# A retention-and-Gelu kernel: the Gelu table loaded at launch, the copies of states spread over ScalarE, VectorE or both, and the casts reordered to match

## The chip, the cores and the metric

One core of a Trainium2 chip. The metric is the device time of one execution in microseconds (us); a kernel's time is the median of several executions. The *span* is what the profiler saw between the first and the last instruction; it is some 1.8 us shorter than the device time. Beside each execution stands the mean clock that was granted to TensorE, where 1.0 is full speed. Times are compared only between executions taken on the same chip. Profiles of several calls, from three chips or more, are set side by side in one table and in some means below; these are compared by stretches, and how far two executions of one kernel differ is shown beside them.

## The reference

```python
# B=8, H=8, S=576, D=64; x becomes 4608 x 512, w_in 512 x 2048, w_out 2048 x 512
def _attn_ref(q, k, v):
    scores = (1 / sqrt(D)) * q @ k.T
    gamma = 1.0 - 2.0 ** (-5.0 - arange(H))
    ret = scores * where(rel >= 0, gamma ** rel, 0.0)      # decay by distance, causal
    return ret @ v

def _moe_ref(x, w_in, w_out):
    h = x @ w_in
    g = 0.5 * h * (1 + tanh(sqrt(2 / pi) * (h + 0.044715 * h ** 3)))
    return g @ w_out

# reference: attention, heads side by side as x, then the two layers
# (the text is shortened: shapes as comments, no type conversions)
```

## The kernel before

The sequence of a batch entry is cut into chunks of 128 rows. What lies within a chunk is computed as scores, a mask and values (`score_mm`, `mask_sc`, `values`); what comes from earlier chunks goes through a state (`state_mm`, then `scan` on VectorE), which is copied by `put` into a block-diagonal float16 tile `tbd` and used by `inter_mm`. `evac` turns the result into `x`. `up` is the first layer with Gelu on ScalarE, `down` the second, as seven products instead of eight with sums and differences prepared by the `mix_` functions.

The program is a list of units of TensorE work; `plan` says after which unit each further step is issued. An instruction queue of an engine runs in the order of issue, so a plan entry decides the place in every queue at once. The letter at the end of an entry is the engine: A is ScalarE, V VectorE, G GpSimd, and S2 splits a copy between A and V.

```python
    def gelu_table():
        nc.scalar.activation(out=p2[:, 3:4], in_=p2[:, 2:3], func=AF.Gelu_apprx_tanh)
# ... cut ...
    def tr(b, s, hh, i, eng):                 # transpose k or q, evacuate to T
        a = att[b]
        t = bank("tr", F16)
        pad(("tr", b, s, hh, i), t)           # dummy matmuls that keep TensorE busy
        # ... cut: four transposes ...
        for e, gs in ((eng, slice(0, 4)),) if eng is not S2 else ((A, slice(0, 2)), (V, slice(2, 4))):
            copy(e, a["T"][:, s, hh, i, gs], src[:, gs])
# ... cut ...
    def put(b, n, eng=None):
        w = att[b]["w", n]
        for hl in range(2):
            copy(eng or nc.scalar, tbd[b % 2][half[hl], n, :, half[hl]], w[half[hl]])
# ... cut ...
    plan = add({},
        (0, L(mask)),
        (0, L(tbd_zero, 0, V)),
        (0, L(cast_qk, 0, 0, 0, "k", A)),
        (0, L(cast_qk, 0, 0, 0, "q", V)),
        (4, L(gelu_table)),
        (0, L(tr, 0, 0, 0, 1, S2)),
        (1, L(score_mm, 0, 0, 0)),
        # ... cut ...
        (8, L(scan, 0, 2)),
        (8, L(put, 0, 2)),
        (8, L(cast_w_in, 0, 1, G)),
        (8, L(cast_w_in, 0, 2, G)),
        (8, L(cast_w_in, 0, 3, G)),
        (8, L(values, 0, 1)),
        (8, L(F0.up_half, 0, 0)),
        (9, L(inter_mm, 0, 1, 1)),
        (10, L(F0.up_half, 1, 0)),
        # ... cut ...
        (78, L(put, 4, 3)),
    )
```

## Time and profile before

| | before |
|---|---|
| median of the first 3 executions | 302.81 us (302.34 to 303.06) |
| span of the profiled execution | 299.4 us |
| first score / last score of the first batch entry | 7.40 / 17.94 us |
| first long run of `up_half` matmuls | 23.43 us |
| first 512-column `up` matmul | 26.05 us |
| first product with w_out | 57.81 us |
| last matmul | 295.69 us |

The events are start times of matmuls, read from the trace. They cut the execution into stretches.

The view of TensorE's waits of the kernel before, from 26 to 128 us (columns: who waited, for whom, total us, how many times, the longest):

```profile
PE hp L555 <- ACT gT L559: 0.5, 1, 0.5
PE st L368 <- ACT T L233: 0.5, 1, 0.5
PE st L368 <- DVE T L233: 0.5, 1, 0.5
PE mu L625 <- DVE ret L381: 0.2, 1, 0.2
PE tr L325 <- DVE vs L446: 0.2, 1, 0.2
```

Only 1.9 us are listed in this long stretch. The first line is the wait at 126 us that the prediction's step (7) is about. Here is its cause, in order of time (columns: start, us, engine, line, operation, what from what; in brackets the idle time before and what ended it):

```profile
123.10 2.52 ACT L233 CAST tbd<-ws 64x256 f16<-64x256 f32 x6 [0.64 <-DVE ws L449]
...
125.64 0.60 ACT L559 ACTIVATE gT<-hp 128x512 f16<-128x512 f32 x1
126.29 3.89 PE L555 MATMUL hp<-x,w_in_sb 128*128 128x512 f16 x16 [0.51 <-ACT gT L559]
```

Six half copies of states stand in ScalarE's queue ahead of a Gelu, and the matmul at 126.29 waits for that Gelu.

### The profile page before, as it was taken

The numbers are of one execution on the slowest core, as the hardware profiler recorded it, in microseconds if no ns is written. First come the engines' busy times: TensorE is split into PE (matmuls) and PEld (weight loads), VectorE is DVE, ScalarE is ACT, GpSimd is POOL, SyncE is SP. The second block draws the span as 40 slices with busy tenths as digits, with TensorE's granted clock in tenths as the row PEclk, the third lists the DMA queues.
The fourth block names the chain that finished last, engine by engine and source line by source line (L and its number), as shares of the span: only waits on it lengthen the run. The fifth ranks groups of instructions, "written<-read, shape, count | busy, mean of one in ns | idle before, by whom it ended". The sixth has DMA issues, their size and how long they took to land.

```text
span 299.4 us, 8730 instructions
## 1 busy us (share of the span) xinstructions
PE 289.7 (97%) x3700; PEld 205.0 (68%) x3700; DVE 218.2 (73%) x416; ACT 163.3 (55%) x318; POOL 79.7 (27%) x108
## 2 busy tenths in 40 slices
PE   8888999999999999999999999999999999999995
PEld 6775577888885568655875587558755874784484
DVE  4776899999998995899559755975598353543434
ACT  6556888875556782665445544554355226505620
POOL 2663564474240343094046006500000000000000
PEclk9999999999999999999999999999999999999999
DMA  7999999758979999985895999491110021003204
GB/s 207 305 337 330 321 387 317 195 131 209 220 235 217 310 237 220 254 276 108 220 308 152 134 258 267 118 137 25 77 66 2 2 83 59 2 1 76 67 0 142
DMA packets 94711, 52.48 MB, mean 175 GB/s; under 512 B 38352, under 2 KB 88528, under 8 KB 94672
## 3 DMA queue, kind: packets, MB, share of 16 engines
q1 hardware_dynamic: 94336, 51.26, 64.4%
q10 hardware_dynamic: 336, 0.66, 0.8%
q8 instruction: 29, 0.48, 0.6%
q14 instruction: 10, 0.08, 0.1%
HBM read 36.70 MB, written 9.44 MB: 154 GB/s over the span
## 4 chain that ended last, share of the span: by engine, by line
PE 76%; DVE 14%; ACT 6%; DMA 2%; issue 1%; DVEq 0%; ACTq 0%
PE hp L555 32%; PE mz L625 8%; PE my L625 8%; PE mu L625 5%; PE mv L625 5%; PE mw L625 4%; PE xs L467 2%; PE hp L568 2%; PE st L368 2%; DMA ld<-in_k_dram 2%; DVE ret L381 2%; DVE ost L652 2%; PE xs L494 2%; ACT tbd L233 2%; DVE w_out_sb L296 1%; ACT gT L559 1%
## 5 line engine op out<-in xcount | busy, mean ns | idle before, releaser
L559 ACT ACTIVATE gT<-hp 128x512 f16<-128x512 f32 x124 | 73.6, 597 | 63.7 <-PE hp L555 62.9
L555 PE MATMUL hp<-x,w_in_sb 128*128 128x512 f16 x432 | 98.7, 379 | 0.6 <-ACT gT L559 0.5
L555 PEld LDWEIGHTS <-w_in_sb 128*128 128x128 f16 x496 | 47.1, 98 | 52.1 <-issue 1.0
L625 PEld LDWEIGHTS <-gT 128*128 128x128 f16 x576 | 55.8, 98 | 8.0
L381 DVE TENSOR_TENSOR ret<-st,cm 128x512 f16<-128x512 f32 x64 | 40.8, 693 | 2.2 <-PE st L368 2.2
L242 POOL TENSOR_TENSOR cv<-ld,sc 128x512 f16<-128x512 f32 x27 | 30.3, 1133 | 28.6 <-DMA ld<-in_v_dram 16.8
L233 ACT CAST tbd<-ws 64x256 f16<-64x256 f32 x64 | 25.8, 403 | 22.2 <-DVE ws L449 19.4
L233 POOL CAST kq<-ld 128x512 f16<-128x512 f32 x24 | 19.4, 810 | 62.0 <-DMA ld<-in_k_dram 46.0
L593 DVE TENSOR_TENSOR gsum<-gT 128x1024 f16<-128x1024 f16 x36 | 26.7, 740 | 12.3 <-ACT gT L559 12.3
L625 PE MATMUL mz<-w_out_sb,gT 128*128 128x256 f16 x288 | 34.4, 273 | 0.0
L625 PE MATMUL my<-w_out_sb,gT 128*128 128x256 f16 x288 | 34.4, 273 | 0.0
L625 PEld LDWEIGHTS <-gsum 128*128 128x128 f16 x288 | 28.0, 98 | 3.5
L652 DVE TENSOR_TENSOR ost<-ost,mv 128x512 f32<-128x512 f32 x18 | 11.5, 682 | 22.3 <-PE mv L625 19.6
L597 DVE TENSOR_TENSOR gT<-gT 128x1024 f16<-128x1024 f16 x36 | 26.9, 751 | 0.5
L507 DVE TENSOR_TENSOR x<-xs,gx 128x512 f16<-128x512 f32 x32 | 21.8, 685 | 6.5 <-PE xs L494 6.4
L585 DVE TENSOR_TENSOR gdia<-gT 128x512 f16<-128x512 f16 (+1 forms) x34 | 17.9, 527 | 10.1 <-ACT gT L559 7.5
L568 PE MATMUL hp<-x,w_in_sb 128*128 128x256 f16 x160 | 18.9, 273 | 0.8 <-DVE x L507 0.8
L233 ACT CAST kq<-ld 128x512 f16<-128x512 f32 x30 | 18.1, 616 | 1.0 <-DMA ld<-in_q_dram 0.7
L625 PE MATMUL mu<-w_out_sb,gsum 128*128 128x256 f16 x144 | 17.2, 273 | 0.2 <-DVE ret L381 0.2
L625 PE MATMUL mv<-w_out_sb,gsum 128*128 128x256 f16 x144 | 17.2, 273 | 0.0
L625 PE MATMUL mw<-w_out_sb,gdia 128*128 128x256 f16 x144 | 17.2, 273 | 0.0
L568 PEld LDWEIGHTS <-w_in_sb 128*128 128x128 f16 x160 | 15.2, 98 | 2.8 <-issue 0.9
(95 smaller groups left out, 319.8 us busy)
## 6 DMA issues: line engine op xcount, KB each, us to landing
ld<-in_k_dram SPq DMA_DIRECT2D x30, 256.0 KB, 5.3
ld<-in_q_dram SPq DMA_DIRECT2D x30, 256.0 KB, 5.3
ld<-in_v_dram SPq DMA_DIRECT2D x30, 256.0 KB, 5.5
out_dram<-ost SPq DMA_DIRECT2D x14, 512.0 KB, 4.6
loan<-in_moe_w_out_dram SPq DMA_DIRECT2D x12, 256.0 KB, 5.4
loan<-in_moe_w_in_dram SPq DMA_DIRECT2D x8, 256.0 KB, 6.1
ld<-in_moe_w_in_dram SPq DMA_DIRECT2D x8, 256.0 KB, 6.0
ld<-in_moe_w_out_dram SPq DMA_DIRECT2D x4, 256.0 KB, 5.6
```

The lines of the kernel that those rows point to most:

```text
L233: (eng.copy if eng is nc.scalar else eng.tensor_copy)(out=out, in_=in_)
L242: eng.tensor_tensor(out=unperm(att[b]["v"][:, s, hh, :]), in0=perm(t), in1=sc[:, 8 * hh : 8 * hh + 8] .rearrange("p (r h) -> p r h", r=2) ...
L381: nc.vector.tensor_tensor(out=x.rearrange("p (a m) -> p a m", a=2), in0=st[hl].rearrange("p (a m) -> p a m", a=2), in1=cm.rearrange("p r s ...
L507: nc.vector.tensor_tensor(out=xb[b][:, :, 2 * s + c].rearrange("p s q i -> p q s i"), in0=att[b]["x", s][c].rearrange("p (q s i) -> p q s ...
L555: nc.tensor.matmul(hp, w_in_sb[:, ct, 128 * f : 128 * f + 128], x[:, :, ct, :], start=(ct == 0), stop=(ct == 3),)
L559: nc.scalar.activation(out=self.g(f // 2)[:, f % 2], in_=hp, func=AF.Gelu_apprx_tanh)
L568: nc.tensor.matmul(hp[:, 256 * h : 256 * h + 256], w_in_sb[:, ct, 256 * j + 128 * h : 256 * j + 128 * h + 128], xb[self.b][:, :, 2 * u : 2 ...
L585: nc.vector.tensor_tensor(out=self.sa[:, j : j + n], in0=g[:, :, 0, 0:256], in1=g[:, :, 1, 256:512], op=ALU.add)
L593: nc.vector.tensor_tensor(out=self.sc[:, j : j + n], in0=g[:, :, 0], in1=g[:, :, 1], op=ALU.add)
L597: nc.vector.tensor_tensor(out=g.rearrange("p j h c -> p j (h c)")[:, :, 256:768].rearrange("p j (h c) -> p j h c", h=2), in0=g[:, :, :, 0: ...
L625: nc.tensor.matmul(o, lhs(j, slice(128 * u, 128 * u + 128)), w_out_sb[:, j, w], start=((u == 0 or isinstance(t, list)) and j == 0 and not ...
L652: nc.vector.tensor_tensor(out=out, in0=in0, in1=t, op=op)
```

## The change

Its intent is to clear ScalarE's queue in the first 27 us, where copies, casts and the table load stood in one row, to give VectorE and GpSimd a share of it, and to do the same for a few places later. It has five parts:

```diff
# 1. the Gelu table at launch; an early dummy Exp starts the Exp table load sooner
     nc.vector.memset(wz, 0.0)
+    nc.scalar.activation(out=p2[:, 3:4], in_=wz[:, 0:1], func=AF.Exp)
...
+    nc.scalar.activation(out=p2[:, 3:4], in_=wz[:, 0:1], func=AF.Gelu_apprx_tanh)
...
-    def gelu_table():
-        nc.scalar.activation(out=p2[:, 3:4], in_=p2[:, 2:3], func=AF.Gelu_apprx_tanh)

# 2. the copy of states names its engine and can be split
-    def put(b, n, eng=None):
+    def put(b, n, eng):
         w = att[b]["w", n]
         for hl in range(2):
-            copy(eng or nc.scalar, tbd[b % 2][half[hl], n, :, half[hl]], w[half[hl]])
+            e = (A, V)[hl] if eng is S2 else eng
+            copy(e, tbd[b % 2][half[hl], n, :, half[hl]], w[half[hl]])

# 3. the start (most entries cut)
+        (0, L(tbd_zero, 0, G)),
+        (0, L(cast_qk, 0, 0, 0, "q", G)),
...
-        (8, L(put, 0, 2)),
+        (8, L(put, 0, 2, V)),
+        (3, L(cast_w_in, 0, 3, A)),
-        (8, L(cast_w_in, 0, 3, G)),
+        (9, L(F0.up_half, 0, 0)),
-        (8, L(F0.up_half, 0, 0)),
...
# 4. casts and sums between 26 and 94 us (cut to three entries), and the last state copy
+        (10, L(cast_w_in, 1, 1, V)),
+        (18, L(cast_w_in, 3, 3, G)),
+        (16, L(cast_v, 1, 0, 0, G)),
...
-        (78, L(put, 4, 3)),
+        (78, L(put, 4, 3, S2)),

# 5. the loop over the later blocks: sums and differences
-            (12, L(F.mix_d, 2, 2)),
+            (13, L(F.mix_d, 2, 2, V)),
-            (11, L(F.mix_sa, 4, 2)),
+            (11, L(F.mix_sa, 4, 2, G)),
...
# and in the last two blocks, five of twelve on GpSimd
+                (4, L(F.mix_sc, 0, 2, G)),
+                (7, L(F.mix_d, 0, 2, G)),
+                (9, L(F.mix_d, 2, 2, G)),
+                (15, L(F.mix_sc, 6, 2, G)),
+                (15, L(F.mix_d, 6, 2, G)),
```

Cut: the order of the first loads, the numbers of dummy matmuls (116 become 128), many moves by one or two units, and a set of new functions (`forms_w`, `pair_a` and so on) that nothing calls, since the list of pairs to use them for is empty.

## The prediction

> **What bounds the kernel now.** I read the page first, then a table of windows by stage, then the chain of waits of the first 27 us, then who waited on TensorE, and last the order of time around each wait. The page's busy shares, with PE at the top:
>
> ```profile
> PE 289.7 (97%) x3700; PEld 205.0 (68%) x3700; DVE 218.2 (73%) x416; ACT 163.3 (55%) x318; POOL 79.7 (27%) x108
> ```
>
> 97% alone doesn't say that TensorE works usefully, so here are stages (columns: window, its length, then busy us and instruction count of PE, PEld, DVE, ACT, POOL, then clock, DMA share, GB/s):
>
> ```profile
> 7.40:15.00 7.60, 6.41 (x169) 5.52 (x170) 5.97 (x12) 4.07 (x8) 4.55 (x7) 1.00 1.10 306
> 15.00:22.00 7.00, 6.29 (x160) 5.11 (x157) 5.48 (x9) 3.46 (x8) 5.08 (x7) 1.00 1.05 334
> 54.00:64.00 10.00, 10.00 (x101) 8.94 (x98) 9.90 (x21) 8.91 (x20) 6.84 (x5) 1.00 0.60 162
> 64.00:78.00 14.00, 13.54 (x233) 11.82 (x232) 13.97 (x28) 6.60 (x15) 6.72 (x8) 1.00 0.80 202
> 154.00:184.00 30.00, 30.00 (x403) 20.40 (x401) 22.03 (x41) 15.78 (x30) 10.04 (x15) 1.00 0.90 213
> 244.00:270.00 26.00, 26.00 (x178) 17.19 (x177) 10.60 (x19) 11.32 (x19) 0.00 (x0) 1.00 0.11 42
> ```
>
> The reader should see three regimes. From 127 us to the last matmul TensorE is full. A block without attention takes 26.03 us, 64 matmuls of 512 columns (13.81 us in the chain of waits) and seven products (1.75 us each, 12.2 us); one with attention 29.9 us. No rearrangement of other engines shortens these 169 us. From 26 to 127 us TensorE has small holes and VectorE is close to full (9.90 of 10 us, 13.97 of 14). Before 26 us TensorE looks busy but does mostly padding: 16 warm-up matmuls (3.59 us) and 116 dummy matmuls of 128 columns, against real work that I estimate at 7.9 us from the counts and shapes. The DMA share there is above 1, at 306 to 334 GB/s. The start is a race between loads and a chain over ACT, DVE and PE:
>
> ```profile
> 11.38 1.28 DVE ret L381 x2
> 12.66 0.34 DVE ws L449
> 13.00 0.02 issue
> 13.02 0.40 ACT tbd L233
> 13.43 0.01 issue
> 13.44 0.40 ACT tbd L233
> 13.84 0.02 issue
> 13.87 0.63 ACT kq L233
> ...
> 14.97 0.59 ACT T L233
> 15.56 0.52 ACT kq L233
> 16.07 0.30 ACT tbd L233
> ...
> 22.08 1.31 DVE x L507 x2
> 23.39 0.04 issue
> 23.43 2.79 PE hp L568 x24
> ```
>
> From 13 to 18 us the chain lies on ScalarE: state copies (tbd), casts of k and q, evacuations of transposes. At 22 to 23.4 us it is two output evacuations on VectorE, behind a late state copy.
>
> **What the Trainium skill says.** "ScalarE: Activation LUTs", section "What ACT_TABLE_LOAD costs", gives about 1283 ns for the load, plus a drain. The trace agrees on the load and shows no separate drain:
>
> ```profile
> 10.76 1.28 ACT L134 ACT_TABLE_LOAD   x1
> 12.05 0.20 ACT L134 ACTIVATE p<-p 128x1 f32<-128x1 f32 x1
> 13.02 0.82 ACT L233 CAST tbd<-ws 64x256 f16<-64x256 f32 x2 [0.77 <-DVE ws L449]
> ```
>
> "TensorE: Matmul & The Clock Gate", section "Back-to-back issue gap", gives N/2.4 + 2.5 ns warm: 216 ns for 512 columns, 109 for 256. The blocks above give 13.81 us / 64 = 216 and 1.75 us / 16 = 109. So the late stages have no TensorE slack. "SBUF — State Buffer", section "Terms", says that VectorE and GpSimd share a port pair under an exclusive lock. The trace agrees as far as casts on GpSimd go: 614 ns undisturbed, but 810 on average over the 24 of the k/q group. "GPSIMD Engine Reference", section "4.1 Engine selection", puts two-input elementwise work at about twice VectorE's time; here the v cast is 1043 ns on GpSimd and 680 on VectorE, a factor of 1.5.
>
> **The change part by part.**
>
> (1) The Gelu table. It removes 1.28 + 0.20 = 1.48 us from ScalarE at 10.76 to 12.25. But the third line above says that ScalarE then idled 0.77 us for VectorE's state (ws), which waited for the mask (ret). The load was hidden: its own worth is 0. At launch, a dummy Exp lets the Exp table load at about 1.05 instead of 1.60, since it waits only for the zero tile. The four gx, sc and gt then end near 4.4 rather than 4.75, and the Gelu load and dummy occupy ScalarE until 5.9. That displaces the first k cast (4.65 on ScalarE).
>
> (2) First casts on GpSimd. After the cm iota (2.53) come four memsets (525 ns each, overlapping, 1.92 us on the trace), to about 4.5. The q cast runs when its load is there (4.80) to 5.4, k to 6.0. Before, both ended near 5.25. The transposes themselves started at 5.72 and 6.33, and the first score at 7.40. With q evacuated by ScalarE (0.59) and k split over both (0.38 and 0.28), I get the score at 7.3: no gain, no loss.
>
> (3) Second heads. Before, the k cast stood behind the first mask on VectorE (mask to 9.15, cast to 9.68) and two transposes followed it. Now k is cast ahead of the mask; only q is behind it (0.43), with one transpose and one evacuation. Four transposes less in series at 56 ns, and a shorter cast: about -0.4 us on the second score, 10.91 to 10.5.
>
> (4) The q cast of the second half moves from ScalarE (0.63 on the chain at 13.87) to GpSimd and can run at its load's landing, about 12.5. Its evacuation is split (-0.2). In return ScalarE takes a weight cast (0.62) after the first state copy. That takes back nearly the cast's share. Together with (3), the last score, 17.94 before, comes near 17.5.
>
> (5) State copy 2 on VectorE. ScalarE did it at 21.38, 0.82 us for two halves, and will now be blocked until about 21.7 by a weight tile that loads late. On VectorE two 64x256 casts cost, from its 128x256 w_out_sb cast at 0.30 us, an estimated 0.6. It delays VectorE's own evacuations, but one of these is no longer behind it: the product with state 1 is issued before the first half product. I estimate VectorE's last evacuation 0.5 us sooner relative to the score. With (3) and (4), the big matmuls begin at 22.5 instead of 23.43: -0.9.
>
> (6) From 26 to 45 us VectorE loses a k cast, a w_in cast (0.42 each), a v cast (0.69) and a q cast (0.79 on the trace), 2.3 us, and gains two w_in casts in its idle time (2.64 us at 24.2) and 0.15 of split evacuations. TensorE's hole at 33.96 (0.46 us wait plus refill) should close: -0.5.
>
> (7) The last state copy before the third block is split. ScalarE had six half copies in a row, 2.52 us, ahead of the Gelu activation at 125.64, for which TensorE waited 0.51 us (126.29). One half less is 0.40: -0.4.
>
> (8) Later blocks: one mix goes to GpSimd, five in the last two, and some subtractions move later. A 1024-element mix there would be 2.1 us by the v cast's rate (an estimate); the last block's two finish near 288.6, and the product that reads the second starts at 292.3. Effect 0. The subtraction moved behind the fourth product ends near 180.9 in the fifth block, 0.2 us before its reader: close, perhaps +0.1 in all.
>
> (9) 128 dummy matmuls instead of 116: 12 x 56 ns = 0.7 us, but inside waits. 0.
>
> Sum: -0.9 - 0.5 - 0.4 + 0.1 = -1.7, and some of it will be lost in the full VectorE stage: -1.6.
>
> **The rivals.** (a) Loads bound. The start's gain is swallowed since the DMA queues are full to 54 us and weights arrive no sooner; the same with VectorE, full from 54 to 94 us. For it: the chain has a 5.74 us load at 44.92, then VectorE work almost without a break to 64.5. Against: (6) relieves VectorE just before. It would give 302.3. (b) Head-of-line blocking. ScalarE has two w_in casts, GpSimd more casts, in queues that run in order; a tile 1 us late stalls TensorE. For it: GpSimd had waits of 4.50 us for w_in and 16.8 in all for v. Against: the load order was moved along with them. It would give 303.5 to 304.5. (c) The whole of the holes goes: the PE waits after 26 us, 3.3 us by summing the start-to-start excess of the larger gaps, and 1.5 at the start. That gives 298.5. (d) Gelu load on the path: 1.48 us more, 299.7; the 0.77 us idle speaks against it.
>
> **Range and chances.** Central 302.8 - 1.6 = 301.2 us. The range runs from between (c) and the sum, 299.5, to just under the time before, 302.8, which includes (a). Two per cent is 6.06 us. Faster by that needs under 296.8, beyond even (c); the start would have to shrink by four microseconds against full DMA queues. Slower by that needs 308.9, several blockings of type (b). Chances: 0.03 faster, 0.96 same, 0.01 slower.
>
> **What would show it.** Right: the table load before 6 us and no gain in the step where it was; second score near 10.5, last near 17.5, first big run of matmuls near 22.5; no TensorE wait near 33 us; the wait at 126 us halved; blocks at 29.9 and 26.03 us as before. Wrong: a TensorE wait for a cast on ACT or POOL between 18 and 36 us (b); the start of the first w_out product unchanged though the start moved (a); a late block longer than 30.0 us, which would put the fault in (8).

## The result, and the profile after

| | before | after |
|---|---|---|
| median | 302.72 us (302.34 to 303.06, 4 executions) | 299.92 us (299.71 to 300.52, 4 executions) |
| ratio of fast executions | | 0.9911 [0.9892, 0.9930] |
| span of the profiled execution | 299.4 us | 298.1 us |
| last matmul | 295.69 us | 294.40 us |

A ratio is the mean time of one kernel's fast executions over that of the other's of the same rounds, so not quite the ratio of the medians; in brackets is its 95% interval. The kernel is faster by 0.9%, within the 2% that counts as the same. Note a trap at once: by the medians it gained 2.8 us, but the two profiles differ by 1.3 us. The profiled execution of the kernel before took 301.22 us, less than any of its four timed ones.

The page of the kernel after, busy us by engine:

```profile
PE 289.9 (97%) x3712; PEld 205.0 (69%) x3712; DVE 217.2 (73%) x400; ACT 160.7 (54%) x316; POOL 108.1 (36%) x130
```

GpSimd works 28 us more, yet VectorE is relieved of only 1.0 us and ScalarE of 2.6. In the last blocks, what moved onto GpSimd slowed VectorE down, as is shown further below. The windows of the kernel after (columns as in the prediction):

```profile
7.40:15.00 7.60, 6.96 (x178) 6.21 (x167) 5.19 (x13) 2.59 (x7) 5.30 (x9) 1.00 1.16 314
...
64.00:78.00 14.00, 13.90 (x242) 12.06 (x243) 13.96 (x27) 6.23 (x14) 9.21 (x12) 1.00 0.97 240
...
244.00:270.00 26.00, 26.00 (x178) 17.16 (x177) 12.42 (x13) 11.28 (x20) 11.36 (x5) 1.00 0.11 42
```

From 7.4 to 15 us ScalarE goes from 4.07 us to 2.59 us of work. From 64 to 78 us VectorE is as full as before, 13.96 of 14 us. In the last window TensorE has no gap, before and after. ScalarE's order of time at the start of the kernel after:

```profile
3.99 1.28 ACT L125 ACT_TABLE_LOAD   x1
5.28 0.20 ACT L125 ACTIVATE p<-wz 128x1 f32<-128x1 f16 x1
5.80 0.99 ACT L232 COPY T<-tr 128x512 f16<-128x512 f16 x2 [0.32 <-PE tr L342]
9.24 0.59 ACT L232 COPY T<-tr 128x512 f16<-128x512 f16 x1 [2.45 <-PE tr L342]
```

The table load and its dummy end at 5.48 us, before ScalarE starts its first evacuation of transposes at 5.80; before the next one it waits 2.45 us for TensorE. The chain of waits up to the first long run, of the kernel after:

```profile
18.73 0.68 DVE ret L408
19.41 0.54 DVE w_in_sb L232
...
20.85 0.28 DVE tbd L232
...
21.15 0.29 DVE tbd L232
...
21.47 1.30 DVE x L535 x2
...
22.81 2.78 PE hp L669 x24
```

The link that was ScalarE's is now two copies of 0.28 and 0.29 us on VectorE, and the evacuations follow with no gap. But VectorE has become the chain from 18.73 us on: even a weight cast (0.54) stands in it.

TensorE's waits in the kernel after, from 26 to 140 us:

```profile
PE hp L669 <- DVE x L535: 0.3, 1, 0.3
PE hp L583 <- DVE ret L408: 0.2, 1, 0.2
PE us L459 <- POOL cv L241: 0.2, 1, 0.2
PE mu L726 <- DVE ret L408: 0.2, 1, 0.2
PE tr L352 <- DVE vs L473: 0.2, 1, 0.2
```

The three waits of 0.5 us are gone; three new ones of 0.2 and 0.3 us have come, and the two behind VectorE's `ret` and `vs` have stayed. At 126 us, now:

```profile
122.15 2.09 ACT L232 CAST tbd<-ws 64x256 f16<-64x256 f32 x5 [0.64 <-DVE ws L476]
...
124.06 0.29 DVE L232 CAST tbd<-ws 64x256 f16<-64x256 f32 x1
124.15 0.59 ACT L587 ACTIVATE gT<-hp 128x512 f16<-128x512 f32 x1
...
124.78 3.97 PE L583 MATMUL hp<-x,w_in_sb 128*128 128x512 f16 x17
```

Five half copies instead of six, the sixth beside them on VectorE; TensorE does not wait at all. One half copy (0.4 us) less was enough to remove a wait of 0.51.

From the first 512-column matmul on, the kernel after stood ahead by 0.62 us (26 us), 0.65 (57 us), 0.95 (105 us), 1.64 (128 us) and 1.29 us from 138 us to the end.

### The profile page after: what moved, and what is told of

Its sections match the earlier page's. It is cut to its first block, busy times and chain, and to the rows that moved or that the text cites. A ratio compares the mean times of both kernels' runs of the same rounds, so it can differ in the third digit from the quotient of the medians.

```text
span 298.1 us, 8776 instructions
## 1 busy us (share of the span) xinstructions
PE 289.9 (97%) x3712; PEld 205.0 (69%) x3712; DVE 217.2 (73%) x400; ACT 160.7 (54%) x316; POOL 108.1 (36%) x130
## 4 chain that ended last, share of the span: by engine, by line
PE 76%; DVE 13%; DMA 5%; SPq 3%; issue 1%; ACT 1%; DVEq 0%
PE hp L583 32%; PE mz L726 9%; PE my L726 9%; PE mu L726 5%; PE mw L726 5%; PE mv L726 4%; PE hp L669 3%; DVE ret L408 3%; DMA loan<-in_moe_w_in_dram 2%; SPq L188 2%; DMA ld<-in_moe_w_out_dram 2%; PE xs L495 2%; PE xs L522 2%; PE st L395 1%; DMA loan<-in_moe_w_out_dram 1%; DVE gT L698 1%
## 5 line engine op out<-in xcount | busy, mean ns | idle before, releaser
L583 PEld LDWEIGHTS <-w_in_sb 128*128 128x128 f16 x496 | 47.1, 98 | 51.8 <-issue 0.7
L232 POOL CAST kq<-ld 128x512 f16<-128x512 f32 x31 | 20.3, 664 | 57.5 <-DMA ld<-in_k_dram 43.2
L241 POOL TENSOR_TENSOR cv<-ld,sc 128x512 f16<-128x512 f32 x28 | 30.9, 1115 | 27.5 <-DMA ld<-in_v_dram 13.2
L232 ACT CAST tbd<-ws 64x256 f16<-64x256 f32 x61 | 24.6, 403 | 23.8 <-DVE ws L476 23.2
L694 DVE TENSOR_TENSOR gsum<-gT 128x1024 f16<-128x1024 f16 x32 | 25.5, 798 | 7.7 <-ACT gT L587 7.7
L694 POOL TENSOR_TENSOR gsum<-gT 128x1024 f16<-128x1024 f16 x4 | 9.2, 2300 | 36.4 <-ACT gT L587 36.4
L686 POOL TENSOR_TENSOR gdia<-gT 128x512 f16<-128x512 f16 x4 | 4.9, 1220 | 37.2 <-ACT gT L587 29.6
L669 PEld LDWEIGHTS <-w_in_sb 128*128 128x128 f16 x160 | 15.3, 98 | 3.4 <-issue 1.5
```

Of the source, the lines that this page charges most:

```text
L232: (eng.copy if eng is nc.scalar else eng.tensor_copy)(out=out, in_=in_)
L241: eng.tensor_tensor(out=unperm(att[b]["v"][:, s, hh, :]), in0=perm(t), in1=sc[:, 8 * hh : 8 * hh + 8] .rearrange("p (r h) -> p r h", r=2) ...
L583: nc.tensor.matmul(hp, w_in_sb[:, ct, 128 * f : 128 * f + 128], x[:, :, ct, :], start=(ct == 0), stop=(ct == 3),)
L669: nc.tensor.matmul(hp[:, 256 * h : 256 * h + 256], w_in_sb[:, ct, 256 * j + 128 * h : 256 * j + 128 * h + 128], xb[self.b][:, :, 2 * u : 2 ...
L686: e.tensor_tensor(out=self.sa[:, j : j + n], in0=g[:, :, 0, 0:256], in1=g[:, :, 1, 256:512], op=ALU.add)
L694: e.tensor_tensor(out=self.sc[:, j : j + n], in0=g[:, :, 0], in1=g[:, :, 1], op=ALU.add)
```

## The experiments

The theories. **By parts:** the start gives about 0.6 us, the split copy at 126 us 0.7 us, the rest of the middle nothing, the later blocks nothing. **Rival 1:** the early Gelu load by itself makes the gain. **Rival 2:** the two executions profiled differ mainly by luck at the start, and much of the 1.3 us is not the kernel's. In this section "before" in a result means the 11 executions of the kernel before on the same chip.

### The kernel before again, unchanged

No edit.

> The kernel before, unchanged: a control. Two profiled runs differ by 1.29 us in span (299.4 and 298.1) but the timed medians by 2.8 us (302.72 and 299.92). Theory A (the profile of before is a lucky execution; its usual span is about 300.9): ratio 1.000, all times 302.3 to 303.1, and the span of this run's profile near 300.9, with the extra 1.5 us at one place. Theory B (the timing of before outside the profile is longer by something after or before the span): ratio 1.000 and span 299.4 again at a time of 302.7.

Measured: 302.66 us (300.95 to 304.12, 6 executions) against 301.97 (301.25 to 302.29), ratio 1.0024 [0.9997, 1.0051]. One and the same kernel spreads over 3.2 us, and even its two sets of executions differ by 0.7 us in the median. Part of the spread lies at one place. TensorE of this execution, in order of time:

```profile
19.26 0.82 PE L467 MATMUL xs<-ret,cv 64*64 64x128 f16 x28
20.82 0.25 PE L467 MATMUL xs<-ret,cv 64*64 64x128 f16 x4 [0.74 <-issue]
21.00 1.05 PE L568 MATMUL hp<-x,w_in_sb 128*128 128x256 f16 x8
```

TensorE stops for 0.74 us after 28 of 32 matmuls of one product. Nothing is waited for ("issue"): these matmuls have all their data. In the profile of the first page the same pause, at the same matmul, is 0.21 us. It is taken up below with the merged dummies.

### The start alone

The kernel before, with the launch, the order of the first loads, the numbers of dummies and all entries up to unit 10 taken from the kernel after.

```diff
+        (8, L(put, 0, 2, V)),
+        (3, L(cast_w_in, 0, 3, A)),
...
# entries from unit 11 on, and the loop: as before
```

> Only the first stage of the change (launch, table load, loads of the first head group and of w_in, dummy matmuls, all steps up to unit 10); everything later as before. Theory C (the gain adds up by stages as the two profiles show): first long run of matmuls at 22.8, 0.6 us sooner, and the time 0.6 us shorter than before, ratio 0.998. Theory D (the 1.5 us that the profiles do not show sit in the start): ratio 0.993, nearly all of the gain. Theory E (the middle stage is bound by VectorE and loads): the start's 0.6 us are lost by 60 us, ratio 1.000.

Measured: 300.39 us, ratio 0.9951 [0.9935, 0.9966]. Its interval excludes 1: the start alone is worth 0.5%. Its profile, span 298.8 us, is ahead of the first profile of the kernel before by only 0.24 us at 26 us and by 0.62 us from 95 us on. Ahead of the profile of the kernel before from the same call it is by 0.74 us at 26 us, by 1.17 at 57 and by 1.48 at the last matmul. The wait at 126 us for a Gelu is still there.

### The middle alone

The kernel before with the entries of units 11 to 78, and the order of the loads behind those of w_in, from the kernel after.

```diff
# units up to 10: as before
...
+        (78, L(put, 4, 3, S2)),
# the loop: as before
```

> Only the steps of units 11 to 78 of the change (with the loads behind w_in), start and late blocks as before. Theory C: the holes at 47.8, 63.9 and 125.6 us close and some new ones open: 0.3 to 1.0 us shorter, ratio 0.998. Theory D: under 0.4 us, ratio 0.999. Theory E: all of the gain, ratio 0.992.

Measured: 300.93 us, ratio 0.9971 [0.9934, 1.0008], unclear by the times. In its profile the stretch with the wait at 126 us is 0.70 us shorter than before. The 31.7 us stretch from 26 to 57 us is not shorter (32.10 us), though the hole at 33 us is closed.

### The loop over the later blocks alone

```diff
-            (11, L(F.mix_sa, 4, 2)),
+            (11, L(F.mix_sa, 4, 2, G)),
...
# everything ahead of the loop: as before
```

> Only the loop over the later blocks as after the change (mixes on GpSimd and later, store later). By both profiles every block past 135 us takes the same time in both kernels, so all theories: ratio 1.000. If not, the 1.5 us lie there. The new TensorE hole of 0.36 us at 132 us should be there if it comes from the mix on GpSimd in the third block, and then the time is 0.3 us longer.

Measured: 301.87 us, ratio 1.0017 [0.9982, 1.0052]. No gain. From 138 us to the last matmul it takes 157.41 us, as does every other kernel.

### The kernel after again, unchanged

> The changed kernel again, as a control beside the controls of before. Theory C (the stage gains of the two single-stage runs, 0.9951 and 0.9971, add up): ratio 0.992, span 297.5 to 299. If it is nearer 0.996, the stages share one gain; nearer 0.988, the chip of the first comparison understated it.

Measured: 300.73 us (299.82 to 301.06, 6 executions) against 302.60 (301.09 to 305.53), ratio 0.9933 [0.9894, 0.9973]. The gain holds, at 0.7%. The ratios of the start alone and the middle alone multiply to 0.992, which lies between the two of the whole change. Here is the most useful table: stretches between the same matmuls in 14 profiles, worked out from start times in the traces (us). "26" is the start of the first 512-column matmul; the next columns are durations from there to the first product with w_out, to the 17th `up` matmul of the block that begins at 91.5 us in the kernel before (at about 95 us), to the 17th of the block that begins there at 123 us (about 127 us), to the 49th of the same block (about 138 us), and to the last matmul.

| kernel, execution | "26" | to 57 | to 95 | to 127 | to 138 | to end |
|---|---|---|---|---|---|---|
| before | 26.05 | 31.76 | 38.08 | 32.40 | 9.99 | 157.42 |
| before again | 26.55 | 31.71 | 38.26 | 32.64 | 9.99 | 157.41 |
| before, dummies merged | 25.91 | 31.83 | 38.25 | 32.40 | 9.99 | 157.42 |
| before, only the Gelu load moved (slow) | 30.74 | 31.38 | 38.44 | 32.81 | 9.99 | 157.42 |
| late part alone | 25.85 | 31.64 | 38.74 | 32.40 | 9.99 | 157.41 |
| start alone | 25.81 | 31.27 | 38.19 | 32.40 | 9.99 | 157.42 |
| middle alone | 25.80 | 32.10 | 38.36 | 31.70 | 9.99 | 157.42 |
| after | 25.43 | 31.73 | 37.78 | 31.70 | 10.34 | 157.41 |
| after again | 26.21 | 32.05 | 37.83 | 31.70 | 9.99 | 157.41 |
| after, state copy 2 on ScalarE | 27.03 | 31.39 | 37.84 | 31.70 | 9.99 | 157.41 |
| after, Gelu load back in the stream | 28.84 | 32.42 | 38.16 | 31.70 | 10.25 | 157.42 |
| after, three edits | 25.42 | 31.80 | 38.50 | 31.71 | 9.99 | 157.42 |
| after, last state copy unsplit | 25.34 | 31.69 | 38.16 | 32.40 | 9.99 | 157.42 |
| after, one mix later | 25.60 | 31.90 | 38.41 | 31.70 | 9.99 | 157.42 |

Three things are to be seen. The last column never moves by more than 0.01 us: no kernel here gains or loses after 138 us. The column "to 127" has two values, 32.40 without and 31.70 with the split copy, with two exceptions, 0.24 and 0.41 us longer, among those without. And the columns "to 57" and "to 95" differ by up to 0.3 us between two executions of one kernel, and by 0.6 to 0.7 ("to 95") among kernels with the same order there, as much as the holes that were to be closed.

That corrects a reading of the first pair of profiles. The wait at 132 us that appeared after the change ("to 138", 10.34 us) is not there when the same kernel runs again. In the first execution, in order of time:

```profile
130.25 1.22 POOL L241 TENSOR_TENSOR cv<-ld,sc 128x512 f16<-128x512 f32 x1
130.49 1.53 DVE L698 TENSOR_TENSOR gT<-gT 128x1024 f16<-128x1024 f16 x1
...
131.94 1.87 DVE L408 TENSOR_TENSOR ret<-st,cm 128x512 f16<-128x512 f32 x3
...
132.67 1.02 PE L583 MATMUL hp<-x,w_in_sb 128*128 128x512 f16 x4 [0.20 <-DVE ret L408]
```

and in the second, which runs 1.14 us later at this point:

```profile
131.61 1.09 DVE L698 TENSOR_TENSOR gT<-gT 128x1024 f16<-128x1024 f16 x1
...
132.12 2.48 POOL L241 TENSOR_TENSOR cv<-ld,sc 128x512 f16<-128x512 f32 x2
132.62 1.87 DVE L408 TENSOR_TENSOR ret<-st,cm 128x512 f16<-128x512 f32 x3
```

The same subtraction on VectorE took 1.53 us where GpSimd began a cast just ahead of it, and 1.09 us where that cast came later. The mask behind it ended in time, and TensorE did not wait. GpSimd's row of casts started at 125.12 us in the first execution and at 127.78 in the second, each time on the landing of a k load.

### The Gelu load alone

The kernel before with parts 1 and 2 of the diff, every copy on ScalarE as before. Four weight casts also changed their places in the list, to other places with the same engine.

```diff
+    nc.scalar.activation(out=p2[:, 3:4], in_=wz[:, 0:1], func=AF.Exp)
...
+    nc.scalar.activation(out=p2[:, 3:4], in_=wz[:, 0:1], func=AF.Gelu_apprx_tanh)
...
-        (4, L(gelu_table)),
```

> Before, with only the two launch-time table loads (dummy Exp and dummy Gelu) and without the step that loaded the Gelu table at unit 4. Theory F (the load was hidden behind the mask and the state on VectorE; my prediction): the second score stays within 0.2 us of 10.9, ratio 1.000 within 0.002; the first k cast on ScalarE moves from 4.65 to about 5.3, so the first score comes 0 to 0.6 us later. Theory G (the table load was on the path): first long run of matmuls 1 us sooner, ratio 0.996.

Measured: 301.62 us, ratio 0.9960 [0.9913, 1.0007], which leaves anything from nothing to 0.9% open. The profiled execution was a slow one (306.21 us, mean clock 0.989), so nothing is read from it after 20 us as a difference between kernels. Up to there it is undisturbed: the second score comes at 10.98 and the last at 18.01 us, against 10.91 and 17.94 before. Taking the load out of the old order moves no event up to there. So this trace gives rival 1 nothing to stand on at the place where the load was. The times can't exclude it: the fast executions at a clock of 0.998 or more have a mean span of 299.62 us against 300.39 for the kernel before.

What this slow execution lost can be seen in it, and that is worth a look though it is no difference between kernels. Windows of this execution (columns as before; the clock is the third number from the right):

```profile
20.00:25.00 5.00, 2.73 (x33) 2.16 (x24) 0.97 (x3) 1.40 (x3) 2.12 (x4) 0.80 1.07 334
25.00:30.00 5.00, 4.05 (x24) 2.91 (x22) 2.50 (x4) 0.60 (x1) 2.25 (x4) 0.52 0.82 244
```

TensorE paused 2.27 us at the place of the pause in "The kernel before again, unchanged", with "issue" as the only reason, and afterwards its clock was half for 6.8 us. That the pause brought the clock down is not shown. The execution was 4.7 us late at the first 512-column matmul.

### The Gelu load back in the stream of the kernel after

```diff
-    nc.scalar.activation(out=p2[:, 3:4], in_=wz[:, 0:1], func=AF.Exp)
...
-    nc.scalar.activation(out=p2[:, 3:4], in_=wz[:, 0:1], func=AF.Gelu_apprx_tanh)
...
+        (4, L(gelu_table)),
# and six weight casts at other places of the list, same engines
```

> The changed kernel with the Gelu load put back in the stream at unit 4, where ScalarE now has put 0, a weight cast and half an evacuation before it. Theory F (hidden): ratio to before still 0.991, milestones as after within 0.2 us. Theory G: 1.3 to 1.5 us longer in the start, the last score near 19.0 instead of 17.66, ratio to before 0.996, since in this order ScalarE carries the chain k cast, state copy 1 and two evacuations right behind it.

Measured: 302.29 us (300.29 to 304.52), ratio 0.9990 [0.9936, 1.0045], against 0.9933 for the kernel after. In executions at a clock of 0.998 or more, the mean span is 299.88 us against 298.60, 1.3 us longer. ScalarE in order of time:

```profile
14.21 0.62 ACT L233 CAST w_in_sb<-loan 128x512 f16<-128x512 f32 x1 [0.91 <-DMA loan<-in_moe_w_in_dram]
14.83 1.28 ACT L134 ACT_TABLE_LOAD   x1
16.12 0.20 ACT L134 ACTIVATE p<-p 128x1 f32<-128x1 f32 x1
16.23 0.35 ACT L233 COPY T<-tr 128x256 f16<-128x256 f16 x1
```

The load that was hidden in the old order stands on the path in the new one: behind the weight cast that ScalarE now does, and in front of the evacuation at 16.23, which is done at 14.31 in the kernel after. The score that needs it starts at 16.97 instead of 15.06 us. Of this, 1.40 us lie between the end of the weight cast and the evacuation, the load and its dummy; the weight cast itself came 0.42 us later than in the kernel after. The later events of this profile are later still, since its clock fell to half from 17.4 to 20.9 us; those are not counted. By these traces the early load is a condition of the new order, not a gain of its own.

### The third state copy back on ScalarE

```diff
-        (8, L(put, 0, 2, V)),
+        (8, L(put, 0, 2, A)),
```

> The changed kernel with state copy 2 of the first batch back on ScalarE, all else as after. Theory H (the move to VectorE is what lets a weight cast that lands at 21.9 stand in ScalarE's queue): the copy now waits behind that cast, to 22.5, the last evacuation ends near 24.4, the first long run starts near 24.4 instead of 22.8, and the ratio to before is 0.996. Theory I (it only swaps 0.82 us on ScalarE for 0.6 on VectorE): 0.2 us, ratio 0.9915.

Measured: 302.61 us, ratio 0.9993 [0.9951, 1.0035]; the whole gain is gone. Three of the six executions had a clock of 0.994. The order of time:

```profile
21.84 0.62 ACT L232 CAST w_in_sb<-loan 128x512 f16<-128x512 f32 x1 [4.11 <-DMA loan<-in_moe_w_in_dram]
...
22.36 0.81 ACT L232 CAST tbd<-ws 64x256 f16<-64x256 f32 x2
...
23.23 0.40 PE L522 MATMUL xs<-T,tbd 128*128 128x128 f16 x4 [1.60 <-ACT tbd L232]
```

ScalarE waits 4.11 us for a weight tile, and the state copy behind it in the queue waits as well, though its data is there at 20.7 us. TensorE loses 1.60 us, and the long run begins 6.62 us after the last score, instead of 5.03 to 5.39 in the six executions of kernels with this start and the copy on VectorE. This single line of the diff is worth about 1.5 us at 23 us, given that the weight cast stands on ScalarE; against the kernel before it is worth less, since there that cast was on GpSimd. Of the loss, 0.3 to 0.7 us is made up again by 57 us (31.39 us in the table). Against the kernel after of the same call this profile is only 0.17 us late at 57 us (58.42 against 58.25) and 0.18 at the last matmul, but it is also the fastest of its six executions. So the stall is shown, and what it costs at the end is known from the times alone. The mean span at full clock is 300.27 us (3 executions) against 298.60.

### The kernel before with its dummies merged

Pairs of 128-column dummy matmuls become one of 256 columns: the same time on TensorE with 48 instructions less. It changes nothing but where in the instruction stream each matmul stands.

```diff
-        for _ in range(pads.pop(key, 0)):
-            if t.dtype == F16:
+        n = pads.pop(key, 0)
+        if t.dtype == F16:
+            for _ in range(n):
...
+        for c in [256] * (n // 2) + [128] * (n % 2):
+            nc.tensor.matmul(t[:, o : o + c], wz[:, 0:128], wz[:, 0:c], start=(o == 0), stop=True, skip_group_check=True)
```

> Before, with each two dummy matmuls of 128 columns that go to an fp32 bank merged into one of 256: the same dummy time, 48 TensorE instructions fewer (24 weight loads, 24 matmuls) ahead of 20 us. In five profiles with this start TensorE paused inside the product of the second half (after the 28th of its 32 matmuls, at 19.5 to 20.2), 0.2 to 2.3 us, waiting for nothing the profile shows, and resumed 1.3 to 1.5 us after a 16 KB packet of the instruction queue had landed. Theory J (TensorE runs out of fetched instructions at a fixed place of its stream): the pause moves 24 matmuls on, so it leaves this product and falls at or near the start of the first long run, where TensorE waits for VectorE anyway; no pause over 0.2 us between 19 and 21, the spans narrower, ratio 0.997. Theory K (the pause comes from the time, or from hidden waits on data): it stays inside that product, ratio 1.000.

Measured: 302.37 us, ratio 1.0009 [0.9972, 1.0046]. TensorE in order of time:

```profile
19.26 0.89 PE L469 MATMUL xs<-ret,cv 64*64 64x128 f16 x32
20.08 1.05 PE L570 MATMUL hp<-x,w_in_sb 128*128 128x256 f16 x8
```

All 32 matmuls run in one piece. This one trace does not prove that the merging took the pause away, since the late part alone, with the old start and its dummies unmerged, has no pause there either (the text above counts five such profiles; it is four). The other traces say more. In the start alone, where the product stands 13 matmuls further down in the stream, TensorE paused 0.15 us after 15 of the 32, which is the same 351st matmul of the stream. So the pause is tied to a place in the stream, not to the data. The traces have a DMA queue of kind "instruction" with 29 packets of 16 KB each (28 in this run). In the kernel before and its twin above, the second packet had landed at 18.89 and 19.54 us, and TensorE went on at 20.31 and 20.82, some 1.3 to 1.4 us later each time; in the slow execution 20.98 and 22.44. In all 14 profiles the 352nd matmul starts 1.29 us or more after this packet has landed: in the five with a pause TensorE came to it sooner, in the nine without it came there later. That TensorE waited for instructions is argued from this agreement; no run moved the packet alone. The time did not get better: the long run begins at 23.29 instead of 23.43 us, since VectorE bounds it.

### Three edits to the kernel after

Aimed at the three new waits of the first profile: the v cast behind weight casts on GpSimd, the sum of w_out on VectorE, the subtraction ahead of the mask.

```diff
-        (18, L(cast_w_in, 3, 3, G)),
+        (20, L(cast_w_in, 3, 3, A)),
...
-        (31, L(mix_w_out, 1, "add", V)),
+        (33, L(mix_w_out, 1, "add", V)),      # further down in the list
...
-            (4, L(F.mix_d, 0, 2, V)),
+            (9, L(F.mix_d, 0, 2, V)),
```

> The changed kernel with three small edits for the TensorE holes that its profile shows: the w_in cast of the fourth group's last tile from GpSimd to ScalarE (hole at 35.2, 0.36 us, behind a v cast on GpSimd), one w_out addition two units later (hole at 49.6, 0.50 us, behind evacuations on VectorE), the first subtraction of the later blocks from unit 4 to 9 (hole at 132, 0.36 us, behind masks on VectorE). Theory C (TensorE alone bounds what follows, holes add up): all three gone, 1.2 us shorter than the changed kernel at the same start, ratio to before 0.988. Theory E (VectorE and loads set the pace to 84 us): the first two come back as holes before 84 us; only the third counts, 0.4 us, ratio 0.991.

Measured: 299.88 us (298.88 to 303.45, the last a slow execution), ratio 0.9923 [0.9882, 0.9964]. It can't be told from the kernel after (0.9911 and 0.9933). In its profile the three waits are gone and others stand at 35.6, 47.1 and 77.9 us (0.43, 0.51 and 0.49 us by the gaps between matmuls), behind masks and an evacuation on VectorE. The unchanged kernel after, run again, has a gap of 0.58 us behind a mask at 36.6 us and no wait at 132 us. The edits moved nothing beyond what an execution moves by itself.

### The last state copy unsplit

```diff
-        (78, L(put, 4, 3, S2)),
+        (78, L(put, 4, 3, A)),
```

> The changed kernel with the last state copy ahead of the third block whole on ScalarE again. My prediction gave the split 0.4 us. If it holds: six half copies in a row on ScalarE again (2.5 us), the wait for the Gelu activation near 125 us 0.4 us longer, and the first matmul of the next unit that much later; in the time too little to be sure of (0.15%). Rival: the loss is made up by the hole at 132 us, which lies behind VectorE and then closes: under 0.1 us from 133 us on.

Measured: 300.67 us (4 executions), ratio 0.9977 [0.9933, 1.0021], against 0.9923 for the three edits. The order of time:

```profile
122.40 2.52 ACT L232 CAST tbd<-ws 64x256 f16<-64x256 f32 x6 [0.64 <-DVE ws L476]
...
125.59 4.75 PE L583 MATMUL hp<-x,w_in_sb 128*128 128x512 f16 x20 [0.51 <-ACT gT L587]
```

Six copies in a row again, and the wait of 0.51 us is back as it was. The stretch "to 127" is 32.40 us. The mean span is 299.18 us, 1.4 us longer than that of the fast executions of the three edits (297.74), with three of the four within 0.4 us and one 1.7 to 2.1 us above them. The split is worth 0.70 us in the traces.

### One mix later

The third of the three edits alone.

> The changed kernel with only the third of the three edits: the first subtraction of the later blocks from unit 4 to unit 9, the middle stage as the change has it. From the runs so far: the hole at 132 us (0.36 us, TensorE behind a mask on VectorE) goes, 0.35 us shorter from 133 us on than at 128 us, nothing else moves. Rival: the subtraction stands then in front of the evacuations of its block and TensorE waits there, 0.2 us or more per block, in four blocks. Ratio to before 0.990 for the first, 0.993 for the second; the time can hardly tell, the trace can.

Measured: 300.82 us (298.91 to 301.54) against 302.18 (301.52 to 304.02), ratio 0.9931 [0.9893, 0.9969]; the kernel after run again had 0.9933. Its profile has no wait at 132 us, but neither has that of the unedited kernel run again, so the run doesn't show that the edit removed it. Instead there is a gap of 0.63 us at 43.2 us, in code that no edit touched. It is one more example of a wait that belongs to an execution and not to a kernel.

No version that was tried beats the kernel after by more than the intervals.

## Why the prediction was right, and where it was not

The predicted time was 301.2 us within 299.5 to 302.8; the measured median was 299.92, inside the range and in the likely class ("same", given 0.96). The gain was 0.9% against 0.5% predicted. That the total fell inside the range is in part luck: the start was put too high, step (6) gave nothing, the split was put too low, and some 0.7 us of the measured gain is in no term of the sum.

**What bounds the kernel.** Right. The section on the issue gap that the prediction cites gives its formula for single matmuls and a shorter distance for a stream of them; here 64 in a row took 216 ns each, as in the formula, and the measurement decides. After 138 us all 14 profiles take 157.41 or 157.42 us to the last matmul. The whole of the change in the profiles is decided before.

**(1) The Gelu load has a worth of 0.** Right in the old order by the trace (no event moved in the run with the load alone, up to 18 us); by the times, anything up to 0.9% stays open. The prediction did not see that the new order needs the move: put back there, the score behind the load came 1.9 us later, of which 1.4 are the load, and the mean span was 1.3 us longer.

**(2), (3) and (4) The scores.** Predicted 7.3, 10.5 and 17.5 us, found 6.99, 10.45 and 17.67. The agreement is chance. The same kernel run again had 7.66, 11.31 and 18.20. In all six profiles with the old start the second score came at 10.51 to 11.03 us, mean 10.87; in the eight with the new one at 10.29 to 11.31, mean 10.74. For the last score the means are 17.90 and 17.84 (without the run that put the Gelu load back). The predicted 0.4 us at either is not there on average. What was sized from durations on VectorE and ScalarE alone did not count that the loads, at a DMA share above 1, and the clock of the first microseconds move these events by more.

**(5) The state copy on VectorE.** The predicted cost of 0.6 us for two halves is what the trace shows, 0.28 and 0.29, and this step carries what the start gains, as far as the traces show. The long run begins on average 5.16 us after the last score in six executions with the new start, and 5.54 in five with the old: 0.4 us. But the prediction had 0.9 us for the whole start, from 23.43 to 22.5, half of it from the scores. Over the same executions the long run begins at 23.02 against 23.41 us, so -0.4 us (22.81 in the first profile). Both pairs of means are of groups that overlap (22.72 to 23.59 against 23.19 to 23.93 us). This is the most oversized term of the sum. In the chain after, VectorE does mask, weight cast, scan, copy and evacuations in one row from 18.73 to 22.77 us without a gap: what ScalarE lost, VectorE took on.

**(6) Minus 0.5 us between 26 and 57 us.** This step failed. The hole named is closed, and VectorE lost the named work, but the stretch is not shorter: 31.73, 32.05, 31.69 and 31.90 us (mean 31.84) against 31.76, 31.71, 31.83 and 31.64 (31.74). Rival (b) happened in the first profile, a cast queued behind weight casts on GpSimd, at 35 us: 0.2 us of wait, 0.36 with refill; the middle part alone shows the same wait with 0.3 us. In other executions of the same order, masks were late instead. VectorE's work from 26 to 45 us fell by 0.85 us (16.76 to 15.91) in the first pair, where the prediction had 2.3. Whether a late start is made up in this stretch is not shown either: starts at 27.03 and 30.74 us had 31.39 and 31.38 us, but one at 28.83 had 32.42, and the shortest, 31.27, followed an early one (25.81). What sets its length was not settled.

**57 to 95 us.** No step gave a gain here. The hole at 63.9 us (0.63 us) is closed with the new middle. Over all executions but the slow one and that of the three edits, the stretch takes 38.08 us on average with the new middle (seven) and 38.30 with the old (five): -0.2 us, beside a spread of 0.6 within each, so not shown.

**(7) The split copy, minus 0.4 us.** The mechanism was right and the size too small: 0.70 us, in every profile with the split, and back to the full amount when it was undone. The prediction counted one copy less (0.40 us). In fact the whole wait of 0.51 us went and with it the rest of the two gaps, of 0.67 and 0.28 us, of which 0.26 us is left by another pair of small gaps.

**(8) Later blocks, plus 0.1 at most.** Right from 138 us on: 0. The wait at 132 us (0.35 us) came in two of the five profiles that have the new middle and the unedited new loop. The estimate of 2.1 us for a 1024-element sum on GpSimd was 2.30 us. But the working missed that it would slow VectorE. From the page after, and two lines of the last block in order of time:

```profile
L698 DVE TENSOR_TENSOR gT<-gT 128x1024 f16<-128x1024 f16 x30 | 27.2, 913 | 0.2
...
L694 POOL TENSOR_TENSOR gsum<-gT 128x1024 f16<-128x1024 f16 x4 | 9.2, 2300 | 36.4 <-ACT gT L587 36.4
```

```profile
283.16 2.36 POOL L694 TENSOR_TENSOR gsum<-gT 128x1024 f16<-128x1024 f16 x1 [2.94 <-ACT gT L587]
...
283.46 2.61 DVE L698 TENSOR_TENSOR gT<-gT 128x1024 f16<-128x1024 f16 x1
```

The same subtraction took 751 ns on average before, and 689 in these last blocks. Beside GpSimd's sum it took 2.61 us, and ended 0.55 us after GpSimd did. Five of twelve operations were moved off VectorE in each of these two blocks, and the 14 that are left took it 15.3 us where 24 took 14.4 before. It cost nothing only because TensorE has no wait there.

**(9) The dummies, 0.** Nothing in the traces speaks against it.

**The sum.** By the means of the stretches the kernel after gains 0.4 us at the start, 0.2 between 57 and 95 us and 0.7 at 126 us, and loses 0.1 up to 57 us and 0.1 at 132 us: 1.1 us in profiled executions, against 1.6 predicted. The timed executions gained more. In all executions, over chips, at a clock of 0.998 or more, the mean span is 300.26 us for the kernel before (45 of them) and 298.42 for the kernel after (10): 1.8 us. In the one call that has many of both it is 1.8 us too (300.39 and 298.60). Executions at a lower clock were 5 of 50 before and 0 of 10 after, which can well be chance. The other 0.7 us is not accounted for by the means of the stretches. Rival 2, luck in the first pair of profiles, is not borne out: in the second pair, of two chips, the last matmuls are 1.37 us apart (296.55 and 295.19), in the first 1.29. The start alone points to where: in the same call its mean span at full clock was 1.4 us shorter than that of the kernel before (298.63 against 300.05); its profile was ahead by 0.6 us of the first profile of the kernel before and by 1.5 of that of its own call, which had the pause of 0.74 us. That pause is a candidate, as the kernel before paused there in both of its profiles and the kernel after in neither. But the kernel with merged dummies, which had no pause at that place in its profile, gained nothing, so the cause stays open.

**What would have shown it wrong.** Of the three signs listed, one came: a TensorE wait for a cast on GpSimd at 35 us, far smaller than rival (b) had it. Rival (a), the gain swallowed behind the start, holds for step (6) and not for (5) and (7). Rival (d), the load on the path before, finds no support in the trace of the run with the load alone; its times don't exclude it. One sum of the prediction is wrong: rival (c), all holes gone, is 302.8 - 3.3 - 1.5 = 298.0, not 298.5 us, so the lower end of the range should have been a little lower.

## What to carry to other kernels

A queue that runs in order is judged by what may block its head: a copy of 0.8 us that TensorE needs must not stand behind a cast whose load may land 4 us late. Here that order stopped TensorE for 1.60 us. Before explaining a wait of a few tenths of a us by a line of the diff, run the same kernel again and compare stretches: here only one of some ten such waits was in every execution of the old order and shortened its stretch in every execution without it. Moving work off an engine need not free it: here ten sums and differences moved to GpSimd left VectorE as busy as before.

## What the Trainium skill lacked or had wrong

- "ScalarE: Activation LUTs", section "What ACT_TABLE_LOAD costs", adds a drain of some 1380 ns to every switch. The traces show 1.28 us for the load and the next activation right behind it (load from 3.99, activation at 5.28 us; load from 14.83, activation at 16.12), with no such time between.
- "SBUF — State Buffer", section "Terms", has the exclusive lock of VectorE and GpSimd, and the runs agree: VectorE's 0.69 us subtraction took 2.61 us beside a 2.36 us sum on GpSimd. That such a move might not help is said in "Perfetto Trace Analysis", section "Optimizing Scalar/DVE Operations". What no page has is a size: moving ten of 24 sums and differences to GpSimd freed no time on VectorE (the 14 left took 15.3 us where all 24 had taken 14.4).
- "GPSIMD Engine Reference", section "4.1 Engine selection", puts two-input work at about twice VectorE's time. For float16 sums of 1024 elements here it is 2300 ns against 689, a factor of 3.3; for the cast with a scale from float32, 1043 against 680 where neither was held up, a factor of 1.5. One factor doesn't serve both.
- "Runtime: NRT & Kernel Launch", section "Instruction fetch mechanics", calls the cost of crossing a 16 KiB block of instructions mostly hidden. No run here proves a wait for instructions, but in five of 14 profiles TensorE paused 0.15 to 2.27 us at one place of the stream, until 1.3 to 1.5 us after a 16 KB packet had landed on the instruction queue, while the DMA queues were full (334 GB/s from 15 to 22 us in the kernel before). The page doesn't say what a full DMA does to it.
- No page gives how much the times of executions of one kernel on one chip differ. Here it is 299.83 to 303.36 us among fast executions, and single waits of 0.2 to 0.6 us come and go among them.
